# Four edits to a planned kernel: PSUM tags of the GT batches, one copy on another engine, later offers of denominators' and M's pieces

## The chip, the cores and the metric

The kernel runs on one core of a Trainium2 chip. The metric is the device time of one execution in microseconds. TensorE (PE) multiplies, VectorE (DVE) and ScalarE (ACT) work element by element, SyncE (SP) and GpSimd (POOL) here issue almost nothing but DMAs. TensorE writes into PSUM alone, which has eight banks; the kernel uses them as four pairs, called ch, dd, cc and rot.

## The reference

A gated mix of two blocks over 2048 tokens of 640 features, all in fp32:

```python
g = sigmoid((x * gate_w).sum(-1, keepdims=True))
# A: linear attention, 32 heads of 20
q, k, v = split(x @ wqkv)
phi = lambda t: where(t > 0, t + 1, exp(t)) + 1e-6
num = phi(q) @ (phi(k)^T v)              # per head
den = phi(q) @ sum_s(phi(k)) + 1e-6      # per head
a = (num / den) @ wo
# B: gated linear unit, F = 1536
b = (sigmoid(x @ w_gate) * (x @ w_up)) @ w_down
out = g * a + (1 - g) * b
```

## The kernel before

**Arithmetic.** Every fp32 operand is split into a high and a low part, and a product is made of three TensorE products, high by high, low by high and high by low (`mm3`, lines 406 to 408 of the profile). A split takes a ScalarE copy (the high part, L419) and a VectorE subtraction (the low part, L423). Larger products use sums of blocks in Strassen's manner (steps s1 to s7), so VectorE also makes sums of tiles.

**Stages, in order of time.** Up to 143 us the keys phi(k) are computed in four chunks of tokens, and the batches of GT = x^T phi(k) are summed into the SBUF tile `gt`. From 143 to 190 us come the queries of the second half of the tokens, and beside them kv = v^T-weight times GT per group of heads (`kv_part`) and M = kv times wo (`m_part`), in six parts hg of 0 to 5. A part of M is two products of 320 columns into two buffers of one PSUM pair, each copied to the tile `ms`, and one store to `m_dram` by POOL's queue. From 190 to 425 us follows the B block for the second half of the tokens, whose weights are split on the way and stored for later; from 425 us the queries and the B block of the first half; from 650 us on the A block's last product, phi(q) / den times M.

**GT batches.** A batch (`GTBatch`) has ten units u, of 128 x 320 outputs each, and up to four token tiles. `part(u, t0, t1, tag)` takes a PSUM buffer of the pair `tag` if the unit has none yet, adds tiles t0 to t1, and, behind the last tile, lets VectorE add the result to `gt`. `ps_tile(tag)` hands out the two buffers of a pair in turn, so the third unit of one tag waits until the first is added. The batches for c of 1, 2 and 3 begin some units earlier, between products of the keys, with two of their four tiles (units 0 to 4 for c of 1, 0 to 3 for c of 2 and 3, in rot, dd, ch and cc); the loop over all ten units then completes them.

**The planner.** The order of every engine's instructions is fixed while the program is built. `Order` keeps an estimated clock for TensorE (`pe`), ScalarE (`act`) and VectorE (`vec`), estimates of when each tile is written and read, and, in `Ring`, of when each DMA lands. Work that isn't tied to a place is offered with `order.add(a, v, fn, key, ready, ...)`: its cost on ScalarE and VectorE, the function that issues it, and a function that says from when it is ready. `order.fill()`, called between products and ahead of each PSUM copy, issues such work while it is ready and its end lies at most a slack behind `pe` (0.6 us for ScalarE, 1.2 for VectorE; 1.6 and 2.4 in some stages). There are several queues: urgent, streams with due times, items, lazy, chain and spare; of the last four only the head may go. `order.need(key)` issues everything up to a key at once. `order.when(tile)` is the estimated time of the tile's last writing, for a DMA its landing. Nothing of this exists at run time: an instruction issued too early simply waits in its engine's queue, and what stands behind it waits too.

**Denominators.** During the B block of the first half, `queue_dens` makes den in a chain for two groups of 512 tokens at a time, queued at block f of 3 (groups 2 and 3) and of 7 (groups 0 and 1). For each group, five pieces `pden` of phi(q) are loaded from `p_dram` by SP, two ahead, and VectorE adds each, times a column of z, to `fac` (`one`, L434 for the first, L427 for the others). Then `fac` goes to `den_dram`, comes back turned (`turn_in`), becomes gate / den (`factor`), goes to `fac_dram` and comes back (`turn_out`). `queue_scale` multiplies with it in the A block.

**M's pieces.** From the end of block 2 of that phase on, `queue_m` loads one of five pieces of M from `m_dram` into the tile `mr` by SP, four DMAs each, splits it into `mt`, and stores it to `mp_dram` by POOL; only then is the next piece queued. They are the spare queue. At block 9 `order.need("m")` makes sure that all are done; then `load_ms` loads into `mt` and `mr` again.

**Down pairs.** In blocks f of 3, 5, 7, 9 and 11 of each B phase, `down_pair` multiplies the gated activations of two blocks (`hf`) by the down weights (`wf` or `wd`), into rot, dd, ch and cc, each output added to `tb` by VectorE (in the first pair copied by ScalarE where `tb` has nothing yet).

Of the kernel before, what the change touches and what calls it, by code (L numbers as in the profile page):

```python
# [9 lines left out]
AF = mybir.ActivationFunctionType  # L10
# [5 lines left out]
S, D, F = 2048, 640, 1536  # L16
H, DH = 32, 20
KC = D // P
# [3 lines left out]
HALF = D // 2  # L22
# [344 lines left out]
def a_cost(w):  # L367
    return 0.06 + w / 1200

def v_cost(w):  # L370
    return 0.07 + w / 960

@with_exitstack
def gated_mix_kernel(ctx: ExitStack, tc: tile.TileContext, xt, xn, wk, wv, wo, wst_q, wst_f, out_t):
# [6 lines left out]
    order = Order()  # L381
# [3 lines left out]
    def f32(ap):  # L385
        return ap.bitcast(F32)

    def width(ap):
        n = 1
        for s in ap.shape[1:]:  # L390
            n *= s
        return n
# [7 lines left out]
    def ps_tile(tag):  # L400
        t = ps_borrow(tag)
        ps_turn[tag] = 1 - ps_turn.get(tag, 0)
        return t

    def mm3(out, l_hi, l_lo, r_hi, r_lo, first, last):
        nc.tensor.matmul(out, l_hi, r_hi, start=first, stop=False, skip_group_check=True)  # L406
        nc.tensor.matmul(out, l_hi, r_lo, start=False, stop=False, skip_group_check=True)  # L407
        nc.tensor.matmul(out, l_lo, r_hi, start=False, stop=last, skip_group_check=True)  # L408
        order.mm(out, width(out), first, l_hi, r_hi)
        order.mm(out, width(out), False, l_hi, r_lo)  # L410
        order.mm(out, width(out), False, l_lo, r_hi)
# [5 lines left out]
    def act(out, src, fn, after="", **kw):  # L417
        order.on_act(width(out), after, out, src)
        nc.scalar.activation(out, src, fn, **kw)  # L419

    def vec2(out, a, b, op, after=""):
        order.on_vec(width(out), after, 1.0, out, a, b)
        nc.vector.tensor_tensor(out, a, b, op=op)  # L423

    def vec3(out, a, scalar, b, op0, op1, after=""):
        order.on_vec(width(out), after, 1.0, out, a, b)
        nc.vector.scalar_tensor_tensor(out, a, scalar, b, op0=op0, op1=op1)  # L427

    def vec1(out, a, s0, s1=None, op0=OP.mult, op1=None, after=""):
        order.on_vec(width(out), after, 1.0, out, a)  # L430
        if op1 is None:
            nc.vector.tensor_scalar(out, a, s0, None, op0=op0)
        else:
            nc.vector.tensor_scalar(out, a, s0, s1, op0=op0, op1=op1)  # L434

    def split(hi, lo, src, after=""):
        act(hi, src, AF.Copy, after)
        at = order.act + A_LAG

        def low():  # L440
            order.vec = max(order.vec, at)
            vec2(lo, src, f32(hi), OP.subtract)
        order.then(low)

    def add(out, a, b, after=""):
        vec2(out, a, b, OP.add, after)
# [10 lines left out]
    fac = common.tile([P, NG, TG], F32, name="fac")  # L457
# [23 lines left out]
    def m1_tile(tag, name, dt=F32, rows=P):  # L481
        return m1.tile([rows, D], dt, name=name, tag=tag, bufs=2 if tag == "ma" else 3)
# [313 lines left out]
    def vec_copy(out, src, after=""):  # L796
        order.on_vec(width(out), after, 1.0, out, src)
        nc.vector.tensor_copy(out, src)
# [222 lines left out]
    g = GTBatch(0, [0])  # L1021
# [8 lines left out]
    for c in range(1, 4):  # L1030
        ck = chunks[c]
        if c == 1:
# [14 lines left out]
            g = GTBatch(c, batches[c])  # L1047
# [97 lines left out]
        if c > 1:  # L1145
            g = GTBatch(c, batches[c])
# [17 lines left out]
            sp.dma_start(w_stage, wst_q[:, KC - 1])  # L1164
            queue_forms(nx)
        for u in range(2 * KC):
            g.part(u, 2 if u in g.ps else 0, 4, ("rot", "dd", "rot", "cc")[u % 4] if c == 3 else "rot")
            order.fill()
            if u in (3, 5, 7, 9,):
                order.run("qw")  # L1170
# [26 lines left out]
    def tt(name, dt=F32, shape=(P, TG)):  # L1197
        return pw.tile(list(shape), dt, name=name, tag="t", bufs=4)
# [202 lines left out]
    def queue_dens(*gs2):  # L1401

        st = {}

        def load(g, u):
            if u < KC:
                st[g, u] = tt("pden")
                sp.dma_start(st[g, u], p_dram[:, u, g])
                st["at", g, u] = lambda: order.when(st[g, u])

        def one(g, u):
            td = fac[:, g]
            if u == 0:
                vec1(td, st[g, u], zcol[:, 0:1], zeps[:, 0:1], OP.mult, OP.add)
            else:
                vec3(td, st[g, u], zcol[:, u:u + 1], td, OP.mult, OP.add)
            load(g, u + 2)
            if u == KC - 1:
                gp.dma_start(den_dram[:, g], td)
                st["at", g, u + 1] = lambda: order.when(den_dram[:, g])  # L1420

        def turn_in(g):
            for j in range(4):
                js = slice(j * H, (j + 1) * H)
                sp.dma_start(fac[js, g].rearrange("h (d c) -> h d c", c=P),
                                  den_dram[:, g, j * P:(j + 1) * P].rearrange("(d h) c -> h d c", h=H))
            st[g, "gs"] = tt("gs")[:, :P]
            sp.dma_start(st[g, "gs"], gate_rep[4 * g:4 * g + 4].rearrange("i h c -> (i h) c"))
            st["at", g, KC + 1] = lambda: max(order.when(fac[:, g]), order.when(st[g, "gs"]))

        def factor(g):
            td = fac[:, g]
            q = td[:, :P]
            add(td[:, :2 * P], td[:, :2 * P], td[:, 2 * P:])
            add(q, q, td[:, P:2 * P])
            order.on_vec(5 * P, "")
            nc.vector.reciprocal(q, q)
            vec2(q, q, st[g, "gs"], OP.mult)
            gp.dma_start(fac_dram[:, g], q)
            st["at", g, KC + 2] = lambda: order.when(fac_dram[:, g])  # L1440

        def turn_out(g):
            for d in range(4):
                sp.dma_start(fac[d * H:(d + 1) * H, g].rearrange("h (j c) -> h j c", c=P),
                                  fac_dram[:, g].rearrange("(j h) c -> h j c", h=H))
        order.add(0, 0, lambda: [load(g, u) for u in range(2) for g in gs2], chain=True)
        for u in range(KC):
            for g in gs2:
                order.add(0, v_cost(TG), lambda g=g, u=u: one(g, u), None, lambda g=g, u=u: st["at", g, u](), chain=True)
        for n, (v, fn) in enumerate(((0, turn_in), (2.0, factor), (0, turn_out))):  # L1450
            for g in gs2:
                order.add(0, v, lambda g=g, fn=fn: fn(g), ("fac", g) if n == 2 else None,
                          lambda g=g, n=n: st["at", g, KC + n](), chain=True)
# [7 lines left out]
    def hg_slice(hg):  # L1461
        h0, h1 = HG[hg:hg + 2]
        return h0 * DH, (h1 - h0) * DH
# [52 lines left out]
    def queue_wo(hg):  # L1516
        if hg < NHG:
            order.add(a_cost(D), v_cost(D), lambda: wo_split(hg), ("wo", hg), lambda: order.when(MO_AT[hg]), first=True)
# [17 lines left out]
    def m_part(hg, tag="cc"):  # L1536
        c0, w = hg_slice(hg)
        order.need(("wo", hg))
        (kvh, kvl), (woh, wol) = KV.pop(hg), WO.pop(hg)
        ms = m1_tile(("ma", "mb")[hg % 2], "ms", F32, bdn)  # L1540
        for h in range(2):
            ps = ps_tile(tag)
            cs = slice(h * HALF, (h + 1) * HALF)
            mm3(ps[:w, :HALF], kvh[:w, :w], kvl[:w, :w], woh[:w, cs], wol[:w, cs], True, True)
            act(ms[:w, cs], ps[:w, :HALF], AF.Copy, "p")
        gp.dma_start(m_dram[c0:c0 + w], ms[:w])
        queue_wo(hg + 2)

# [122 lines left out]
    def m_rows(dst, cols, queue, u=None):  # L1671

        for d in range(4):
            m = m_dram.rearrange("(h u d) n -> d h u n", u=KC, d=4)[d]
            queue.dma_start(dst[d * H:(d + 1) * H], m[:, u] if cols is None else m[:, :, cols])

    def queue_m(u=0):

        raw = down_pool[1].tile([P, D], F32, name="mr", tag="mr")
        m_rows(raw, None, sp, u)  # L1680

        def fn():
            t = down_pool[1].tile([P, 2, D], F32R, name="mt", tag="mt")
            split(t[:, 0], t[:, 1], raw)

            def rest():
                gp.dma_start(mp_dram[:, u], f32(t))
                if u + 1 < KC:
                    queue_m(u + 1)
            order.then(rest)  # L1690
        order.add(a_cost(D), v_cost(D), fn, "m", lambda: order.when(raw), spare=True)

    def m_close():
        nonlocal tb
# [499 lines left out]
    for hg, (j, t) in enumerate(((5, "cc"), (6, "dd"), (8, "dd"), (10, "dd"), (12, "dd"), (13, "dd"))):  # L2194
        extra[j].append(lambda hg=hg, t=t: m_part(hg, t))
# [427 lines left out]
```

## Time and profile before

| | us |
|---|---|
| median of 3 runs | 733.24 (733.22 to 734.12) |
| the profiled execution, whole | 733.22 |
| its span, first to last instruction | 731.3 |
| TensorE busy | 726.0 |
| VectorE busy | 561.3 |
| ScalarE busy | 358.4 |
| granted TensorE clock | 1.0 |

Rows in order of time give start, duration, engine, line, operation, output<-inputs, shape and count; in brackets is the idle time before the instruction and what ended it. Instructions of one kind that follow each other are merged into one row with a count. Rows of a tile give durations in ns as least/median/most, then the first and the last start in us. A row of waits gives the waiting engine and tile, what it waited for, the total in us, how many times, and the longest. A row of a stretch has its length, then busy us and instructions of PE, PEld (weight loads), DVE, ACT and POOL, the granted clock, the DMA share and GB/s. L406 to L408 are `mm3`'s three products, L419 any ScalarE activation, L423 any two-tensor VectorE operation, L427 its three-operand form, L798 a VectorE copy, L363 any DMA.

### The profile page before, as it was taken

Reading aid. Unit: us, or ns where it says so; the run is one execution under the profiler, and the core shown is the slowest. Engines: PE = TensorE matmul, PEld = TensorE weight load, DVE = VectorE, ACT = ScalarE, POOL = GpSimd, SP = SyncE. Lnnn points to the kernel's source line nnn. Section 1 sums busy time; section 2 is a strip of 40 time slices with the busy share of each in tenths; the row PEclk is TensorE's granted clock in tenths of the full one; section 3 lists DMA queues with packets and bytes.
Section 4 is the critical chain, followed back from the end, with each engine's and each line's share of the span. In section 5 each row is a group of like instructions: output and inputs, shape, how many; then the busy total and the mean of one; then the engine's idle time right before and its main releaser. Section 6 shows DMA issues by size and latency. Waiting matters only on the chain.

```text
span 731.3 us, 10111 instructions
## 1 busy us (share of the span) xinstructions
PE 726.0 (99%) x3575; PEld 622.6 (85%) x3575; DVE 561.3 (77%) x987; ACT 358.4 (49%) x668; POOL 94.7 (13%) x161
## 2 busy tenths in 40 slices
PE   9999999999999999999999999999999999999997
PEld 7999999988888888888888888887888888888886
DVE  4978787987677889898989973456685867698783
ACT  5765647357556653535355363454333232334550
POOL 0211111113211211211210031001000041000000
PEclk9999999999999999999999999999999999999999
DMA  7564747697887866457687288878879697859212
GB/s 260 131 187 123 188 112 240 157 348 273 285 297 259 329 240 234 187 216 261 251 324 264 103 289 331 310 257 296 284 271 334 213 325 211 297 217 340 82 63 102
DMA packets 71945, 173.54 MB, mean 237 GB/s; under 512 B 11690, under 2 KB 33466, under 8 KB 68310
## 3 DMA queue, kind: packets, MB, share of 16 engines
q1 hardware_dynamic: 55526, 109.99, 45.6%
q0 software_dynamic: 16224, 62.74, 24.3%
q8 instruction: 28, 0.46, 0.2%
q14 instruction: 23, 0.19, 0.1%
q10 hardware_dynamic: 144, 0.16, 0.1%
HBM read 103.96 MB, written 63.92 MB: 230 GB/s over the span
## 4 chain that ended last, share of the span: by engine, by line
PE 85%; DVE 5%; DMA 4%; issue 2%; ACT 2%; POOL 1%; SPq 0%; DVEq 0%; POOLq 0%; ACTq 0%
PE ch L406 9%; PE ch L407 9%; PE ch L408 9%; PE cc L406 8%; PE cc L408 8%; PE cc L407 8%; PE dd L406 6%; PE dd L407 6%; PE dd L408 6%; PE rot L406 5%; PE rot L408 5%; PE rot L407 5%; DMA wo_sb<-wo 1%; DMA pden<-p_dram 1%; DVE gt L423 1%
## 5 line engine op out<-in xcount | busy, mean ns | idle before, releaser
L419 ACT ACTIVATE c<-ch 128x512 f32<-128x512 f32 x52 | 31.0, 597 | 94.0 <-PE ch L408 93.8
L423 DVE TENSOR_TENSOR hf<-c,hf 128x512 fp32r<-128x512 f32 x75 | 51.1, 687 | 25.5 <-ACT hf L419 25.0
L419 ACT ACTIVATE hf<-c 128x512 fp32r<-128x512 f32 x75 | 46.0, 624 | 26.7 <-DVE c L423 26.6
L423 DVE TENSOR_TENSOR c<-cc,c 128x512 f32<-128x512 f32 x40 | 27.6, 689 | 38.6 <-PE cc L408 24.8
L406 PE MATMUL ch<-xth,ws 128*128 128x512 f32 x112 | 43.7, 390 | 0.0
L407 PE MATMUL ch<-xtl,ws 128*128 128x512 f32 x112 | 43.6, 389 | 0.0
L408 PE MATMUL ch<-xth,ws 128*128 128x512 f32 x112 | 43.6, 389 | 0.0
L423 DVE TENSOR_TENSOR tb<-rot,tb 128x512 f32<-128x512 f32 (+1 forms) x61 | 39.2, 672 | 3.0 <-PE rot L408 3.0
L423 DVE TENSOR_TENSOR tb<-dd,tb 128x512 f32<-128x512 f32 x44 | 30.1, 685 | 8.7 <-PE dd L408 8.7
L406 PE MATMUL dd<-xrh,wg 128*128 128x512 f32 x90 | 35.2, 391 | 0.0
L408 PE MATMUL dd<-xrh,wg 128*128 128x512 f32 x90 | 35.0, 389 | 0.0
L407 PE MATMUL dd<-xrl,wg 128*128 128x512 f32 x90 | 35.0, 389 | 0.0
L423 DVE TENSOR_TENSOR c<-c,c 128x512 f32<-128x512 f32 x46 | 31.6, 687 | 2.6 <-ACT c L419 2.0
L419 ACT ACTIVATE c<-dd 128x512 f32<-128x512 f32 x22 | 13.1, 597 | 41.7 <-PE dd L408 41.5
L407 PE MATMUL cc<-xbl,ws 128*128 128x512 f32 x84 | 32.7, 389 | 0.0
L406 PE MATMUL cc<-xbh,ws 128*128 128x512 f32 x84 | 32.7, 389 | 0.0
L408 PE MATMUL cc<-xbh,ws 128*128 128x512 f32 x84 | 32.7, 389 | 0.0
L419 ACT ACTIVATE dd<-ch 128x512 f32<-128x512 f32 x22 | 12.8, 582 | 33.4 <-PE ch L408 33.4
L423 DVE TENSOR_TENSOR wst<-wst 128x256 f32<-128x256 f32 (+2 forms) x69 | 27.4, 412 | 1.4
L406 PE MATMUL rot<-pkh,xnh 128*128 128x320 f32 x90 | 28.1, 312 | 0.1
L407 PE MATMUL rot<-pkl,xnh 128*128 128x320 f32 x90 | 27.8, 309 | 0.0
L408 PE MATMUL rot<-pkh,xnl 128*128 128x320 f32 x90 | 27.8, 309 | 0.0
(648 smaller groups left out, 2327.8 us busy)
## 6 DMA issues: line engine op xcount, KB each, us to landing
wf<-ws POOLq DMA_DIRECT2D x12, 1152.0 KB, 7.6
ws<-wf SPq DMA_DIRECT2D x11, 1152.0 KB, 8.4
wst<-wst_f SPq DMA_DIRECT2D x12, 640.0 KB, 5.1
wf<-wg POOLq DMA_DIRECT2D x12, 640.0 KB, 6.7
wd<-wd POOLq DMA_DIRECT2D x12, 640.0 KB, 8.3
wg<-wf SPq DMA_DIRECT2D x12, 640.0 KB, 5.5
wf<-wd SPq DMA_DIRECT2D x10, 640.0 KB, 9.3
xnst<-xn SPq DMA_DIRECT2D x16, 320.0 KB, 4.1
```

The lines of the kernel that those rows point to most:

```text
L406: nc.tensor.matmul(out, l_hi, r_hi, start=first, stop=False, skip_group_check=True)
L407: nc.tensor.matmul(out, l_hi, r_lo, start=False, stop=False, skip_group_check=True)
L408: nc.tensor.matmul(out, l_lo, r_hi, start=False, stop=last, skip_group_check=True)
L419: nc.scalar.activation(out, src, fn, **kw)
L423: nc.vector.tensor_tensor(out, a, b, op=op)
```

## The change

In the loop over the ten units, batches for c of 1 and 2 now take their tags in turn from rot, dd, rot, cc for units under 8, as the batch for c of 3 did for all ten; units that have a buffer already keep it. The fifth part of M (hg of 4) is copied out of PSUM by VectorE, both halves; the other five parts stay with ScalarE. A denominators' piece is offered 1.5 us behind the modelled landing of its load, the factor 2.5 us behind the modelled landing of its two inputs, a piece of M 2 us behind that of its load.

```diff
         for u in range(2 * KC):
-            g.part(u, 2 if u in g.ps else 0, 4, ("rot", "dd", "rot", "cc")[u % 4] if c == 3 else "rot")
+            g.part(u, 2 if u in g.ps else 0, 4, ("rot", "dd", "rot", "cc")[u % 4] if c == 3 or u < 8 else "rot")
             order.fill()
...
                 sp.dma_start(st[g, u], p_dram[:, u, g])
-                st["at", g, u] = lambda: order.when(st[g, u])
+                st["at", g, u] = lambda: order.when(st[g, u]) + 1.5
...
-            st["at", g, KC + 1] = lambda: max(order.when(fac[:, g]), order.when(st[g, "gs"]))
+            st["at", g, KC + 1] = lambda: max(order.when(fac[:, g]), order.when(st[g, "gs"])) + 2.5
...
             mm3(ps[:w, :HALF], kvh[:w, :w], kvl[:w, :w], woh[:w, cs], wol[:w, cs], True, True)
-            act(ms[:w, cs], ps[:w, :HALF], AF.Copy, "p")
+            if hg == 4:
+                vec_copy(ms[:w, cs], ps[:w, :HALF], "p")
+            else:
+                act(ms[:w, cs], ps[:w, :HALF], AF.Copy, "p")
         gp.dma_start(m_dram[c0:c0 + w], ms[:w])
...
-        order.add(a_cost(D), v_cost(D), fn, "m", lambda: order.when(raw), spare=True)
+        order.add(a_cost(D), v_cost(D), fn, "m", lambda: order.when(raw) + 2, spare=True)
```

## The prediction

> **What bounds the kernel now.** I read the head of the page first, then TensorE's list of waits, then the table by stretches, and then the order of time around each wait.
>
> ```profile
> span 731.3 us, 10111 instructions
> PE 726.0 (99%) x3575; PEld 622.6 (85%) x3575; DVE 561.3 (77%) x987; ACT 358.4 (49%) x668; POOL 94.7 (13%) x161
> ```
> ```profile
> PE rot L494 <- PEq L2614: 0.8, 1, 0.8
> PE rot L406 <- DVE tb L423: 0.4, 1, 0.4
> PE dd L406 <- ACT ms L419: 0.2, 1, 0.2
> ```
> ```profile
> 625.00:732.00 107.00, 102.59 (x467) 85.33 (x465) 78.19 (x129) 41.74 (x78) 0.00 (x0) 1.00 0.49 175
> ```
>
> TensorE is the bound. It is idle for 731.3 - 726.0 = 5.3 us: 0.8 before its first product, some 3.7 behind its last one (625.00 to 731.3 is 106.3 us, of which it is busy 102.59), and the rest in a few waits. No product is added or dropped, so the change can gain only what TensorE loses in waits, and it can lose time only by making new ones. Since busy spans overlap and are modelled, I measure a wait by the distance from one start to the next, against that distance where nothing waits. The profiled execution took 733.22 us, 0.02 below the median of the runs (733.24), so its span and the 1.9 us around it can be used as they are.
>
> **GT batches in four banks.** Only units 5 and 7 of the second and third batch (c of 1 and 2) get another tag: the first batch has a loop of its own, for c of 3 the four tags are there already, units 0 to 3 have their buffer by then, and 4 and 6 keep rot.
>
> ```profile
> 62.83 0.31 PE L407 MATMUL rot<-pkl,xnh 128*128 128x320 f32 x1
> 62.98 0.31 PE L408 MATMUL rot<-pkh,xnl 128*128 128x320 f32 x1
> 63.41 0.41 PE L406 MATMUL rot<-pkh,xnh 128*128 128x320 f32 x1
> 63.66 0.31 PE L407 MATMUL rot<-pkl,xnh 128*128 128x320 f32 x1
> ```
> ```profile
> 58.63 0.48 DVE L423 TENSOR_TENSOR gt<-rot,gt 128x320 f32<-128x320 f32 x1
> ...
> 62.27 0.69 DVE L423 TENSOR_TENSOR xst<-xst 128x512 f32<-128x512 f32 x1
> 62.87 0.48 DVE L423 TENSOR_TENSOR gt<-rot,gt 128x320 f32<-128x320 f32 x1
> ```
>
> The regular distance is 62.98 - 62.83 = 0.15 us. At 63.41 unit 8 of the batch for c = 1 begins, after 0.43 instead, and its second product after 0.25: 0.28 + 0.10 = 0.38 us lost. It waits for a rot buffer. There are two, so unit 8 takes the one of unit 6, whose add stands on VectorE behind an x sum and starts only at 62.87. With the new tags unit 5 goes to dd and unit 7 to cc; unit 8 then takes the buffer of unit 4, added at 58.63, and unit 9 that of unit 6, added by 63.35, when unit 8 is just begun. The dd and cc buffers come free at adds that stand ahead of these in program order. VectorE's work stays the same, and what is next late is the x forms of the following chunk. I count the whole 0.38. The batch for c = 2 shows no wait: nothing to gain, and what hides the edit is that its adds keep up.
>
> **M's fifth part copied by VectorE.**
>
> ```profile
> 178.69 0.31 PE L408 MATMUL dd<-woh,kvl 100*100 100x320 f32 x1
> 180.21 0.39 PE L407 MATMUL ch<-xtl,ws 128*128 128x512 f32 x1
> 180.44 0.40 PE L408 MATMUL ch<-xth,ws 128*128 128x512 f32 x1
> 181.04 0.39 PE L406 MATMUL dd<-woh,kvh 100*100 100x320 f32 x1 [0.21 <-ACT ms L419]
> 181.27 0.31 PE L407 MATMUL dd<-wol,kvh 100*100 100x320 f32 x1
> ```
> ```profile
> 189.51 0.39 PE L406 MATMUL ch<-xth,ws 128*128 128x512 f32 x1
> ```
> ```profile
> 179.42 1.25 ACT L419 ACTIVATE ws<-wst 128x640 fp32r<-128x640 f32 x2
> 180.57 0.74 ACT L419 ACTIVATE ms<-dd 100x320 f32<-100x320 f32 x2
> ```
> ```profile
> 178.98 0.82 DVE L432 TENSOR_SCALAR zperm<-zacc 128x640 f32<-128x640 f32 x1
> 179.71 0.68 DVE L427 SCALAR_TENSOR_TENSOR qe<-qe,c 128x512 f32<-128x512 f32 x1
> 180.31 1.42 DVE L423 TENSOR_TENSOR ws<-wst,ws 128x640 fp32r<-128x640 f32 x2
> 181.84 0.69 DVE L423 TENSOR_TENSOR c<-cc,c 128x512 f32<-128x512 f32 x1
> 183.89 0.69 DVE L427 SCALAR_TENSOR_TENSOR qe<-qe,c 128x512 f32<-128x512 f32 x1 [1.36 <-ACT c L419]
> ```
> ```profile
> L798 DVE COPY gt<-dd x3: 475/477/479, 25.5 to 29.5; 128x320 f32<-128x320 f32 x3
> L419 ACT ACTIVATE gt<-dd x2: 437/438/438, 29.1 to 31.2; 128x320 f32<-128x320 f32 x2
> ```
>
> The regular distance here is 180.44 - 180.21 = 0.23, behind a 320-wide product 0.15. The sixth part starts after 0.60, and its second product after 0.23: 0.37 + 0.08 = 0.45 us lost. It waits for the copy of the fifth part's first half. That half's last product ended at 179.00, but its copy stands on ScalarE behind two weight splits until 180.57. On VectorE the two copies can stand ahead of the column permutation, from about 179.05 to 180.0, which frees the buffer some 0.7 us before it is wanted at 180.67. The price is two copies of 477 ns each, 0.95 us, against two of 438 on ScalarE. Behind them are queued the permutation, one phi step and the two halves of the ws low parts, which end at 181.73 now and at about 182.7 then. TensorE first reads that tile at 189.51, 6.8 us later, and VectorE's next gap of 1.36 us takes up the delay. The store of this part on POOL's queue goes out sooner, not later. So 0.45 gained, and nothing paid as long as those 6.8 us are there.
>
> The Trainium skill speaks against this edit: "Advanced Engine Details and Errata" says in its list of workarounds that ScalarE is the engine closer to PSUM, and "Perfetto Trace Analysis", section Optimizing Scalar/DVE Operations, gives about 125 ns of access overhead to a VectorE instruction on PSUM and about 51 to a ScalarE one. By that page two copies would cost 2 x 74 = 0.15 us more on VectorE, an estimate; the two gt rows above, the same shape on both engines, say 2 x 39 = 0.08 us. By either the sum is the same, because the copies lie beside TensorE's work.
>
> **Denominators' and M's pieces offered later.**
>
> ```profile
> 495.76 0.39 PE L408 MATMUL dd<-hf,wf 128*128 128x512 f32 x1
> 496.54 0.50 PE L406 MATMUL rot<-hf,wf 128*128 128x512 f32 x1 [0.39 <-DVE tb L423]
> 496.87 0.39 PE L407 MATMUL rot<-hf,wf 128*128 128x512 f32 x1
> ```
> ```profile
> 492.72 2.07 DVE L427 SCALAR_TENSOR_TENSOR fac<-pden,zcol,fac 128x512 f32<-128x512 f32 x3
> 495.13 0.75 DVE L427 SCALAR_TENSOR_TENSOR fac<-pden,zcol,fac 128x512 f32<-128x512 f32 x1 [0.34 <-DMA pden<-p_dram]
> 495.80 1.28 DVE L423 TENSOR_TENSOR tb<-rot,tb 128x512 f32<-128x512 f32 x2
> ```
> ```profile
> 497.97 0.74 ACT L419 ACTIVATE mt<-mr 128x640 fp32r<-128x640 f32 x1 [4.59 <-DMA mr<-m_dram]
> ```
> ```profile
> L427 DVE SCALAR_TENSOR_TENSOR fac<-pden,zcol,fac x16: 739/744/752, 489.2 to 587.7; 128x512 f32<-128x512 f32 x16
> ...
> L363 SPq DMA_DIRECT2D fac<-fac_dram x16: 309/436/687, 540.1 to 621.1; - x16
> ...
> L427 DVE SCALAR_TENSOR_TENSOR hf<-hf,fac x10: 682/683/686, 669.6 to 676.0; 128x512 f32<-128x512 f32 x10
> ```
> ```profile
> L363 POOL DMA_DIRECT2D mt<-m_dram x8: 574/574/617, 589.4 to 596.0; - x8
> ...
> L363 POOL DMA_DIRECT2D mp_dram<-mt x5: 532/538/540, 492.5 to 538.0; - x5
> ```
> ```profile
> 591.92 0.39 PE L406 MATMUL dd<-hf,wf 128*128 128x512 f32 x1
> ```
>
> TensorE's longest wait inside the program: 0.78 against 0.23, then 0.33 against 0.23, so 0.55 + 0.10 = 0.65 us lost. The adds that free rot stand on VectorE behind four denominators' pieces, the last of which waits 0.34 us for its own load. Of the 0.65, 0.34 is that wait and the rest is the pieces themselves. Offered 1.5 us behind the modelled landing, a piece no longer holds VectorE for a load; whether the adds also come ahead of it is the planner's choice. Bounds: 0 (the pieces bunch elsewhere) to 0.65; I take 0.65, because each of the pieces ahead moves as well, the later ones by two such delays.
>
> What the delays push back: five rounds a group at 1.5 us are at most 7.5 us, and the factors 2.5 more, 10 us in all. The last turned factors are issued at 621.1 now, by 631 then, and first multiplied at 669.6. M's pieces: five at 2 us, so the last store goes from 538.0 to 548, and the mt tile is wanted again at 589.4. SP's loads of pieces and POOL's stores move with them; no weight load stands behind a wait that is longer than before, since SP issues the next piece's load when the piece has been used, and that now waits less. ScalarE's wait of 4.59 us at 497.97 shrinks by about 2, which gains nothing: TensorE runs on through it. One thing comes nearer: the second set's last piece starts at 587.7, and the next down pair, where a piece can stand before an add as at 496.54, begins at 591.92. A shift beyond some 3.5 us puts one or two pieces into it.
>
> The sum: 733.22 - 0.38 - 0.45 - 0.65 = 731.74 us.
>
> **Rivals.** *The denominators' wait only moves.* GT's and M's waits go, but one or two pieces fall before an add in this pair or in that at 591.92, at 0.65 each: 733.22 - 0.83 + 0 to 0.65 = 732.4 to 733.0. For it: the 7.5 us above against 3.5. Against it: a piece whose data is there costs 0.7 us of VectorE and not a wait, and behind an add it costs nothing.
>
> *Pieces bunch before the adds (slower).* The head of the chain is held back, and then several pieces are ready at once, as the three from 492.72 are, and go out where the planner thinks that VectorE has room. It reckons 512/960 + 0.07 = 0.60 us for a piece whose row says 0.74, so a bunch of four overruns by over 0.5 us. The twenty pieces pass through three down pairs. The estimate: with none of the 0.65 gained and five new waits of that size, 733.22 - 0.83 + 3.25 = 735.6. It decides from (0.83 + 1.47) / 0.65 = 3.5, so four waits on. Any other reordering that the changed estimates bring into the long middle part would have to cost as much. Against it: sixteen of the twenty pieces cost TensorE nothing before.
>
> *The edits don't reach the waits.* If the copies are placed on VectorE behind the ws low parts, or unit 8 still meets a full buffer, there is no change: 733.2.
>
> **How the numbers follow.** A measurement of this kernel can tell about 0.2% from no change, 1.47 us; the forecast gain of 1.48 lies on that line. All three waits go: 0.58, of which I put 0.44 beyond the line (small gaps also close) and 0.14 within. The wait only moves: 0.20, within. The edits miss: 0.02, within. Bunching: 0.20, slower. The time is that of the first case, 731.7. The range goes from 731.2 (0.5 below it: the runs before spread over 0.9) to 734.4, which takes in the second and third rival and bunching with three new waits (732.4 + 1.95); the rest of bunching is left out.
>
> **What would show it.** Right: TensorE's list of waits keeps only the start; two 100x320 copies by VectorE from about 179; no VectorE wait on pden; the last M store near 545, the last turned factors before 635. Wrong: a TensorE wait on tb or gt anywhere between 480 and 625, or new waits between 182 and 480, where there are none.

## The result and the profile after

| | before | after |
|---|---|---|
| median of 12 runs each, us | 733.65 (733.19 to 735.91) | 731.78 (731.41 to 732.20) |
| the profiled execution, whole | 733.22 | 731.51 |
| its span | 731.3 | 729.6 |

The ratio is 0.9972, with an interval of 0.9963 to 0.9981: faster by 1.87 us, against a forecast of 1.48. Run again beside the later experiments, the change took 731.80 against 734.14, a ratio of 0.9967 [0.9955, 0.9980].

The head of the page after, and the whole of TensorE's list of waits:

```profile
span 729.6 us, 10115 instructions
PE 725.0 (99%) x3575; PEld 623.4 (85%) x3575; DVE 562.3 (77%) x989; ACT 357.8 (49%) x666; POOL 94.9 (13%) x161
```
```profile
PE rot L494 <- PEq L2617: 0.8, 1, 0.8
```

VectorE has two instructions more and ScalarE two fewer, the two copies of M's fifth part. TensorE's products are the same 3575, and of the three waits only the start is left. The three places of the prediction, in TensorE's order of time:

```profile
62.70 0.31 PE L408 MATMUL cc<-pkh,xnl 128*128 128x320 f32 x1
62.84 0.31 PE L406 MATMUL rot<-pkh,xnh 128*128 128x320 f32 x1
62.99 0.31 PE L407 MATMUL rot<-pkl,xnh 128*128 128x320 f32 x1
...
179.78 0.39 PE L408 MATMUL ch<-xth,ws 128*128 128x512 f32 x1
180.01 0.32 PE L406 MATMUL dd<-woh,kvh 100*100 100x320 f32 x1
180.17 0.31 PE L407 MATMUL dd<-wol,kvh 100*100 100x320 f32 x1
...
494.74 0.39 PE L408 MATMUL dd<-hf,wf 128*128 128x512 f32 x1
494.97 0.39 PE L406 MATMUL rot<-hf,wf 128*128 128x512 f32 x1
495.19 0.39 PE L407 MATMUL rot<-hf,wf 128*128 128x512 f32 x1
```

The distances are now the regular ones: 0.14 and 0.15 us at unit 8 of the batch, 0.23 and 0.16 at M's sixth part, 0.23 and 0.22 at the product into rot. With the products of both traces put side by side, start against start, the gain grows as follows: 0.28 us by the time of 30 us, where no edit has acted yet (this differs from one execution to the next); 0.38 more at unit 8; 0.45 more at M's sixth part, of which 0.06 is given back just behind it; 0.66 more near 495. From there to the end it stays between 1.68 and 1.72, and the two spans differ by 1.71.

What VectorE does at the second of these places:

```profile
178.38 0.93 DVE L798 COPY ms<-dd 100x320 f32<-100x320 f32 x2
179.23 0.82 DVE L432 TENSOR_SCALAR zperm<-zacc 128x640 f32<-128x640 f32 x1
179.96 0.69 DVE L427 SCALAR_TENSOR_TENSOR qe<-qe,c 128x512 f32<-128x512 f32 x1
180.56 1.43 DVE L423 TENSOR_TENSOR ws<-wst,ws 128x640 fp32r<-128x640 f32 x2
...
183.95 0.69 DVE L427 SCALAR_TENSOR_TENSOR qe<-qe,c 128x512 f32<-128x512 f32 x1 [1.36 <-ACT c L419]
```

The copies stand ahead of the permutation, as supposed, and the ws low parts end at 181.99, far ahead of their reading; the gap of 1.36 us ahead of the phi step (L427) is as long as before. And at the third:

```profile
487.55 1.22 DVE L434 TENSOR_SCALAR fac<-pden,zcol,zeps 128x512 f32<-128x512 f32 x2 [1.57 <-DMA pden<-p_dram]
...
490.29 1.41 DVE L427 SCALAR_TENSOR_TENSOR fac<-pden,zcol,fac 128x512 f32<-128x512 f32 x2
491.92 0.75 DVE L427 SCALAR_TENSOR_TENSOR fac<-pden,zcol,fac 128x512 f32<-128x512 f32 x1 [0.22 <-DMA pden<-p_dram]
492.98 0.75 DVE L427 SCALAR_TENSOR_TENSOR fac<-pden,zcol,fac 128x512 f32<-128x512 f32 x1 [0.31 <-DMA pden<-p_dram]
493.65 1.28 DVE L423 TENSOR_TENSOR tb<-rot,tb 128x512 f32<-128x512 f32 x2
```

The kernel before began this stretch so:

```profile
487.75 1.22 DVE L434 TENSOR_SCALAR fac<-pden,zcol,zeps 128x512 f32<-128x512 f32 x2 [0.76 <-DMA pden<-p_dram]
489.18 0.75 DVE L427 SCALAR_TENSOR_TENSOR fac<-pden,zcol,fac 128x512 f32<-128x512 f32 x1 [0.21 <-DMA pden<-p_dram]
490.71 0.75 DVE L427 SCALAR_TENSOR_TENSOR fac<-pden,zcol,fac 128x512 f32<-128x512 f32 x1 [0.78 <-DMA pden<-p_dram]
```

Before, six pieces by L427 stood between the two first ones (L434) and the two rot adds: those at 489.18 and 490.71, three from 492.72 and one at 495.13. Now there are four. The adds begin at 493.65 instead of 495.80; 1.02 of these 2.15 us had been gained ahead of this place, and the other 1.13 are more than the 0.55 that TensorE stood waiting, so TensorE finds its buffer free. VectorE still waits for loads: the brackets in the rows after show 1.57, 0.22 and 0.31 us.

From the answers by tile, for pden (first before, then after), fac, mt and ms:

```profile
  DMA pden<-p_dram: 2.1, 4
```
```profile
  DMA pden<-p_dram: 2.1, 3
```
```profile
L363 SPq DMA_DIRECT2D fac<-fac_dram x16: 309/430/1082, 538.4 to 619.0; - x16
```
```profile
L363 POOL DMA_DIRECT2D mp_dram<-mt x5: 534/540/540, 490.1 to 538.3; - x5
```
```profile
L419 ACT ACTIVATE ms<-dd x8: 420/436/442, 164.2 to 181.1; 100x320 f32<-100x320 f32 x6, 120x320 f32<-120x320 f32 x2
L798 DVE COPY ms<-dd x2: 492/493/494, 178.4 to 178.8; 100x320 f32<-100x320 f32 x2
```

The first two rows say that VectorE's waits on pden come to 2.1 us before and after, in 4 places and in 3. The last turned factors are issued at 619.0 (621.1 before) and the last store of M at 538.3 (538.0 before). TensorE is 1.7 us ahead of the kernel before by then, so against its work the factors come 0.4 us sooner and the store 2.0 later; both are far from the 10 us that were reckoned.

### The profile page after: what moved, and what is told of

The parts are those of the page before. It is cut to its first block, busy times and chain, and to the rows that moved or that the text cites. A ratio compares the mean times of both kernels' runs of the same rounds, so it can differ in the third digit from the quotient of the medians.

```text
span 729.6 us, 10115 instructions
## 1 busy us (share of the span) xinstructions
PE 725.0 (99%) x3575; PEld 623.4 (85%) x3575; DVE 562.3 (77%) x989; ACT 357.8 (49%) x666; POOL 94.9 (13%) x161
## 4 chain that ended last, share of the span: by engine, by line
PE 99%; DVE 0%; issue 0%
PE ch L406 11%; PE ch L407 11%; PE ch L408 11%; PE cc L406 9%; PE cc L407 9%; PE cc L408 9%; PE dd L406 8%; PE dd L407 8%; PE dd L408 8%; PE rot L406 6%; PE rot L407 6%; PE rot L408 6%; PE rot L1525 1%; PE rot L494 0%; PE ch L965 0%; PE dd L965 0%
## 5 line engine op out<-in xcount | busy, mean ns | idle before, releaser
L408 PEld LDWEIGHTS ch<-xth,ws 128*128 128x128 f32 x112 | 21.0, 188 | 4.7 <-DVE ws L423 0.3
L407 PEld LDWEIGHTS ch<-xtl,ws 128*128 128x128 f32 x112 | 21.0, 188 | 4.2
L406 PEld LDWEIGHTS ch<-xth,ws 128*128 128x128 f32 x112 | 21.0, 188 | 4.1
```

## The experiments

Twelve kernels in three groups, each group timed beside the kernel before (medians 734.17, 734.26 and 734.14). What TensorE lost at each place in the profiled execution, in us, worked out from distances of starts as in the prediction:

| | GT unit 8 | M | near 496 | near 518 | near 530 | span |
|---|---|---|---|---|---|---|
| before | 0.38 | 0.46 | 0.66 | 0 | 0 | 731.3 |
| GT alone | 0 | 0.47 | 0.89 | 0 | 0 | 731.6 |
| M's fifth part alone | 0.38 | 0.02 | 1.96 | 0 | 0 | 731.8 |
| denominators alone | 0.39 | 0.46 | 0 | 0.78 | 1.39 | 732.7 |
| M's pieces alone | 0.44 | 0.47 | 1.59 | 0.28 | 0 | 732.6 |
| denominators and M's pieces | 0.38 | 0.46 | 0 | 0 | 0 | 731.0 |
| all but M's pieces | 0 | 0.02 | 0 | 0 | 1.11 | 731.3 |
| all | 0 | 0.01 | 0 | 0 | 0 | 729.6 |

The spans hold something else besides: from TensorE's start to the first GT product the executions take 21.5 to 22.4 us, a difference of up to 0.9, so they are no measure of a few tenths.

### GT's tags alone

```diff
-            g.part(u, 2 if u in g.ps else 0, 4, ("rot", "dd", "rot", "cc")[u % 4] if c == 3 else "rot")
+            g.part(u, 2 if u in g.ps else 0, 4, ("rot", "dd", "rot", "cc")[u % 4] if c == 3 or u < 8 else "rot")
```

> Only the GT batches' tags are changed, all else as before. Theory (each edit removes one wait, and they add up): the wait at unit 8 of the batch for c = 1 goes, 0.38 us, the waits near 181 and 496 stay; 0.4 us faster than before, no new wait. Rival (VectorE is the bound in that batch and the wait only moves): a TensorE wait on another PSUM pair or on an x form between 63 and 75 us, no gain.

Measured: 733.37 us, ratio 0.9990 [0.9979, 1.0002]. The interval includes 1, so the time alone doesn't show the forecast 0.4 us. In the trace the wait at unit 8 goes from 0.38 to 0, and no other appears between 63 and 75 us. The profiled execution loses this gain again: 0.21 us at 160.5, where the kernel before loses nothing and the profile names no releaser, and 0.23 at the wait near 496, which is longer here (TensorE's order of time):

```profile
495.74 0.39 PE L408 MATMUL dd<-hf,wf 128*128 128x512 f32 x1
496.75 0.50 PE L406 MATMUL rot<-hf,wf 128*128 128x512 f32 x1 [0.62 <-DVE tb L423]
```

### M's fifth part alone

```diff
-            act(ms[:w, cs], ps[:w, :HALF], AF.Copy, "p")
+            if hg == 4:
+                vec_copy(ms[:w, cs], ps[:w, :HALF], "p")
+            else:
+                act(ms[:w, cs], ps[:w, :HALF], AF.Copy, "p")
```

> Only M's fifth part is copied by VectorE. Theory: the wait near 181 us goes, 0.45 us faster than before, VectorE's copies start about when the products end and the weights' low parts end some 1 us later without TensorE noticing. Rival (a copy on VectorE costs more there than it saves, because what is queued behind it is late): gain under 0.2 us, with a TensorE wait between 181 and 195.

Measured: 733.70 us, ratio 0.9999 [0.9989, 1.0008]. The wait at M's sixth part goes, 0.46 to 0.02, and yet no gain shows in the time; the interval would hide one of up to 0.8 us, so the trace has to say where it went. TensorE's and VectorE's order of time near 496:

```profile
494.97 0.39 PE L408 MATMUL dd<-hf,wf 128*128 128x512 f32 x1
497.05 0.50 PE L406 MATMUL rot<-hf,wf 128*128 128x512 f32 x1 [1.69 <-DVE tb L423]
```
```profile
488.54 1.21 DVE L434 TENSOR_SCALAR fac<-pden,zcol,zeps 128x512 f32<-128x512 f32 x2 [2.34 <-DMA pden<-p_dram]
...
496.31 1.28 DVE L423 TENSOR_TENSOR tb<-rot,tb 128x512 f32<-128x512 f32 x2
```

TensorE comes to the last product into dd 0.8 us sooner than before (494.97 against 495.76; about half of it is this edit, the rest the start of this execution) and starts the next one 0.5 us later (497.05 against 496.54). VectorE has stood waiting for its first pieces until 488.54, 0.79 later than before, and the adds are 0.51 later (496.31 against 495.80). In this execution the end of the wait is set by loads, not by how early TensorE comes.

### The denominators' delays alone

```diff
-                st["at", g, u] = lambda: order.when(st[g, u])
+                st["at", g, u] = lambda: order.when(st[g, u]) + 1.5
...
-            st["at", g, KC + 1] = lambda: max(order.when(fac[:, g]), order.when(st[g, "gs"]))
+            st["at", g, KC + 1] = lambda: max(order.when(fac[:, g]), order.when(st[g, "gs"])) + 2.5
```

> Only the denominators' pieces and factors are offered later (1.5 and 2.5 us). Theory: the wait near 496 us goes, 0.65 us faster than before, because fewer pieces stand ahead of the two adds into tb on VectorE. Rival (M's pieces hold VectorE and ScalarE there): the wait stays at 0.4 us or more.

Measured: 734.24 us, ratio 0.9997 [0.9987, 1.0008]. The wait near 496 is gone, and two others have come: 0.78 us near 518, of which the list of waits puts 0.4 on a weight load (`wf<-wd`), and 1.39 near 530. The second, in the order of time of TensorE, ScalarE and VectorE:

```profile
529.72 0.39 PE L408 MATMUL cc<-hf,wf 128*128 128x512 f32 x1
531.23 0.50 PE L406 MATMUL rot<-hf,wf 128*128 128x512 f32 x1 [1.11 <-DVE tb L423]
```
```profile
528.38 0.74 ACT L419 ACTIVATE mt<-mr 128x640 fp32r<-128x640 f32 x1 [5.18 <-DMA mr<-m_dram]
```
```profile
529.15 0.83 DVE L423 TENSOR_TENSOR mt<-mr,mt 128x640 fp32r<-128x640 f32 x1 [2.39 <-ACT mt L419]
...
530.49 1.28 DVE L423 TENSOR_TENSOR tb<-rot,tb 128x512 f32<-128x512 f32 x2
```

A piece of M is split ahead of the rot adds. ScalarE waits 5.18 us for its load, VectorE 2.39 for ScalarE, the adds stand behind that, and TensorE waits for the adds.

### M's pieces' delay alone

```diff
-        order.add(a_cost(D), v_cost(D), fn, "m", lambda: order.when(raw), spare=True)
+        order.add(a_cost(D), v_cost(D), fn, "m", lambda: order.when(raw) + 2, spare=True)
```

> Only M's pieces are offered later (2 us). Theory: TensorE never waited for them, and six denominators' pieces still stand ahead of the two adds: the wait near 496 us stays at 0.5 to 0.7 us and the time is that of before within 0.1 us. Rival (the split of M's piece is what holds the adds up): the wait shrinks by half or more, 0.3 to 0.6 us faster.

Measured: 737.84 us (734.33 to 739.04), ratio 1.0048 [1.0033, 1.0063]: slower, which no theory gave. Its profiled execution was the fastest of its runs, 734.33, and shows 1.59 us near 496, as in the old order, and 0.28 near 518. Against the kernel before these are 1.2 us more, about what the two profiled executions differ by (1.1). There are six runs instead of twelve. The other 3.5 us, from this execution to the median, were not seen in a trace, and what they are stays open.

### Denominators' and M's pieces together, without the first two edits

```diff
-                st["at", g, u] = lambda: order.when(st[g, u])
+                st["at", g, u] = lambda: order.when(st[g, u]) + 1.5
...
-        order.add(a_cost(D), v_cost(D), fn, "m", lambda: order.when(raw), spare=True)
+        order.add(a_cost(D), v_cost(D), fn, "m", lambda: order.when(raw) + 2, spare=True)
```

(and the factor's 2.5)

> Both kinds of offers later (denominators' 1.5 and 2.5 us, M's pieces 2 us), GT tags and M's fifth part as before. Theory after the first runs (the two work only together: the first empties VectorE's queue ahead of the adds near 496, the second keeps a split of M's piece out of the next down pair, where it held an add for 1.4 us at 530): no TensorE wait between 480 and 560, 0.7 to 1.5 us faster than before, and a spread over the runs under 1.5 us. Rival (each acts alone, as at first thought): the wait at 530 is there again and nothing is gained.

Measured: 732.49 us, ratio 0.9971 [0.9957, 0.9985]. No wait of TensorE from 480 to 560, and the runs lie within 1.0 us. Alone, the one edit gives nothing that can be measured and the other loses; together they gain 1.8 us.

### The whole change without the delay of M's pieces

```diff
-        order.add(a_cost(D), v_cost(D), fn, "m", lambda: order.when(raw) + 2, spare=True)
+        order.add(a_cost(D), v_cost(D), fn, "m", lambda: order.when(raw), spare=True)
```

> The whole change without the later offer of M's pieces. Theory: GT's and M's waits are gone (0.37 and 0.4 us), the wait near 496 too, but a split of M's piece stands ahead of two adds near 530 and costs 1 to 1.5 us: slower than the whole change by 1 to 2 us, at the time of before or up to 0.5 us under it. Rival (M's offers don't matter): the time of the whole change within 0.3 us.

Measured: 732.89 us, ratio 0.9977 [0.9965, 0.9990], about 1.1 us above the whole change (731.80, in the third group, where the kernel before took 734.14 instead of 734.26). The intervals of the two ratios overlap, so the times alone don't decide it; the traces do. TensorE and VectorE near 530, first of this kernel, then VectorE of the whole change:

```profile
529.80 0.50 PE L406 MATMUL rot<-hf,wf 128*128 128x512 f32 x1 [0.83 <-DVE tb L423]
```
```profile
527.72 0.83 DVE L423 TENSOR_TENSOR mt<-mr,mt 128x640 fp32r<-128x640 f32 x1 [2.11 <-ACT mt L419]
...
529.07 1.28 DVE L423 TENSOR_TENSOR tb<-rot,tb 128x512 f32<-128x512 f32 x2
```
```profile
527.01 1.28 DVE L423 TENSOR_TENSOR tb<-rot,tb 128x512 f32<-128x512 f32 x2
```

With the 2 us the piece of M goes to another place, and the adds come 2.06 us sooner; 0.51 of that is the whole change's lead in its own execution. The loss near 530 is in both profiled kernels that delay the denominators without M's pieces (1.39 and 1.11 us) and in none that delays both. So the delay that the prediction counted at nothing is what keeps the denominators' gain.

### Only unit 5, or only unit 7, on another pair

Each kernel was run once, so there is no interval, and the reading rests on the order in the trace. In both, the batch for c of 3 stays as it was.

```diff
+ only unit 5: ("rot", "dd", "rot", "cc")[u % 4] if c == 3 else "dd" if u == 5 else "rot"
+ only unit 7: ("rot", "dd", "rot", "cc")[u % 4] if c == 3 else "cc" if u == 7 else "rot"
```

> Of the whole change only unit 5's tag in the GT batches for c = 1 and 2 (to dd). Unit 8 then still takes the buffer of unit 6. By the prediction's account (the buffer alone decides) the wait at unit 8 stays at some 0.4 us. Rival: the planner also puts unit 6's add ahead of the x sum on VectorE, a microsecond earlier, and that alone removes the wait.

> Of the whole change only unit 7's tag in the GT batches for c = 1 and 2 (to cc). Unit 8 then takes the buffer of unit 5, and unit 6's add stays behind the x sum. By the prediction's account the wait at unit 8 goes, 0.38 us. Rival (only the earlier add helps): it stays.

With unit 5 alone (one run, 733.85 us) unit 8 still takes the buffer of unit 6, and still doesn't wait. VectorE and TensorE:

```profile
62.31 0.48 DVE L423 TENSOR_TENSOR gt<-rot,gt 128x320 f32<-128x320 f32 x1
62.71 1.41 DVE L423 TENSOR_TENSOR xst<-xst 128x512 f32<-128x512 f32 x2
```
```profile
63.19 0.31 PE L408 MATMUL rot<-pkh,xnl 128*128 128x320 f32 x1
63.33 0.31 PE L406 MATMUL rot<-pkh,xnh 128*128 128x320 f32 x1
```

The planner has put unit 6's add ahead of the x sums, at 62.31 instead of 62.87, and that is enough. With unit 7 alone (one run, 733.53) the add stays behind an x sum, and unit 8 takes the other buffer:

```profile
61.81 0.68 DVE L423 TENSOR_TENSOR xst<-xst 128x512 f32<-128x512 f32 x1
62.41 0.48 DVE L423 TENSOR_TENSOR gt<-rot,gt 128x320 f32<-128x320 f32 x1
```
```profile
62.53 0.31 PE L408 MATMUL cc<-pkh,xnl 128*128 128x320 f32 x1
62.67 0.31 PE L406 MATMUL rot<-pkh,xnh 128*128 128x320 f32 x1
```

Unit 8 starts 0.14 behind the product ahead of it, at 62.67, while that add is still running. Either means alone is enough.

### The change again

> The whole change again, beside the runs of this job. Theory: the three waits stay gone in every run, so the spread is under 1.5 us, and the ratio to before is 0.996 to 0.998; before's runs spread wider because the landing of the denominators' loads near 490 differs from run to run.

Measured: 731.80 us (731.40 to 732.56), profiled 731.75, span 729.8, TensorE losing nothing at the five places of the table but 0.02 at M.

### Denominators' pieces offered 4 us late

```diff
-                st["at", g, u] = lambda: order.when(st[g, u]) + 1.5
+                st["at", g, u] = lambda: order.when(st[g, u]) + 4
```

> The whole change, with denominators' pieces offered 4 us behind their modelled landing instead of 1.5. Theory: VectorE's waits on these loads (2.1 us in the profile before) fall under 0.7, one piece stands between the two adds near 494, TensorE doesn't wait, and the time is that of the whole change within 0.4 us. Rival (the prediction's slower case: pieces held back bunch ahead of the adds of the down pairs): TensorE waits on tb between 490 and 610, 0.6 us each, 0.6 to 2 us slower than the whole change.

Measured: 731.70 us, ratio 0.9958 [0.9945, 0.9971], the same as the whole change. From the answers on pden and fac:

```profile
  DMA pden<-p_dram: 0.4, 1
```
```profile
L427 DVE SCALAR_TENSOR_TENSOR fac<-pden,zcol,fac x16: 739/744/748, 491.6 to 597.7; 128x512 f32<-128x512 f32 x16
```

VectorE waits 0.4 us for these loads instead of 2.1, and the last piece starts at 597.7, within the pair that begins near 590 here (591.92 before). TensorE has no wait either way. So pieces in that pair cost nothing here, they don't bunch to a loss, and VectorE's wait on pden is not itself what costs: it did so only where the adds stood behind it and TensorE had come to their buffer.

### All six parts of M copied by VectorE

```diff
-            if hg == 4:
-                vec_copy(ms[:w, cs], ps[:w, :HALF], "p")
-            else:
-                act(ms[:w, cs], ps[:w, :HALF], AF.Copy, "p")
+            vec_copy(ms[:w, cs], ps[:w, :HALF], "p")
```

> The whole change, with all six parts of M copied by VectorE. Theory (the fifth part gains only because ScalarE's queue is full there and VectorE's is not): ten more copies of 0.48 us make VectorE late somewhere between 155 and 195, a TensorE wait of 0.3 to 2 us in all, slower than the whole change by as much. Rival (VectorE is simply the better engine for this copy): no new wait, the time of the whole change within 0.3 us.

Measured: 732.47 us (731.63 to 734.24), ratio 0.9975 [0.9961, 0.9989]. The stretch from 155 to 195 us of the whole change and of this kernel:

```profile
155.00:195.00 40.00, 40.00 (x213) 34.30 (x212) 29.57 (x56) 28.17 (x52) 12.08 (x22) 1.00 0.90 319
```
```profile
155.00:195.00 40.00, 40.00 (x212) 33.94 (x211) 33.82 (x68) 24.85 (x42) 12.08 (x22) 1.00 0.90 311
```

VectorE is busy for 33.82 of the 40 us instead of 29.57, and TensorE for all 40 in both. The list of waits has nothing new, and the span is 729.8, but the order of time holds one small wait of the expected kind. VectorE's add of a cc buffer into c runs from 182.25 to 182.93, where the whole change has it from 181.90 to 182.59. The first product into that pair starts at 182.99, lasts 0.50 us instead of 0.39, and the next follows after 0.33 instead of 0.23: 0.15 us lost, against 0.3 to 2 expected. So VectorE's lead is just used up there. The median is 0.67 above the whole change, with a wider spread and overlapping intervals; what makes up the rest isn't settled.

### The first GT batch in four pairs too

The first batch waits as well: its units start late near 30 and 31 us, 0.41 us in all in the profile after.

```diff
-                g.part(u, 0, 2, "rot" if u % 2 else "dd")
+                g.part(u, 0, 2, ("dd", "rot", "ch", "cc")[u % 4])
```

> The whole change, and the first GT batch, too, turns in four PSUM pairs (dd, rot, ch, cc instead of dd and rot). Theory: the two waits left there, near 30 and 31 us (0.2 to 0.3 and 0.17 us), go: 0.3 to 0.5 us faster than the whole change. Rival (what is behind those waits is late too): the wait moves to the key products that follow at 32, no gain.

Measured: 731.46 us (730.92 to 733.21), ratio 0.9962 [0.9948, 0.9975]. The waits near 30 and 31 us are gone, 0.41 to 0.00; in its profiled execution 0.30 is lost near 519, for which the list of waits names no cause. By its median it is the fastest of all, 0.34 below the change, but the intervals don't tell the two apart.

## Why the prediction was right, and where it was not

**GT, 0.38.** Measured 0.38. The account, that the buffer decides, is half of it: an earlier place of unit 6's add does the same with the buffer unchanged (the run with unit 5 alone), and VectorE's order after the whole change has both:

```profile
61.82 0.48 DVE L423 TENSOR_TENSOR gt<-rot,gt 128x320 f32<-128x320 f32 x1
62.22 1.41 DVE L423 TENSOR_TENSOR xst<-xst 128x512 f32<-128x512 f32 x2
```

The prediction took VectorE's order as given where the new tags had moved it.

**M's fifth part, 0.45.** Measured 0.45, of which 0.06 is given back. The copies began at 178.38 and the low parts of ws ended at 181.99. Against the forecast of 179.05 and 182.7 that is 0.7 us sooner, but TensorE was 0.65 us ahead of the kernel before at that place: the forecast of the order was right to within 0.1. The two copies take 493 ns each against 436 on ScalarE, a difference of 57; with all six parts on VectorE ten such copies take 480 at the median, 44 more. The Trainium skill, "Perfetto Trace Analysis", section Optimizing Scalar/DVE Operations, gives 125 ns of access against 51, a difference of 74. The trace agrees in direction and comes out smaller, though the rows are whole durations and not the access alone. As the prediction said, by either the time is the same, since the copies lie beside TensorE's work. That holds for one part; with all six, 0.15 us of it reached TensorE.

**Denominators, 0.65.** Measured 0.66 between the two traces. But the size belongs to the one execution from which it was taken. Six profiled executions have the old order on VectorE at this place: the kernel before, GT's tags alone, M's fifth part alone, M's pieces alone, unit 5 and unit 7. TensorE was ready for this product at 495.2 to 496.0 us, and the product started at 496.5 to 497.4; the two earliest arrivals (495.2 and 495.3) started at 497.1 and 496.8, no sooner than the others. The loss was 0.66 in the kernel before and 0.89, 1.96, 1.59, 0.98 and 1.64 in the others. This is the term that was mis-sized for the median: the median gain was 1.87 and 2.34 us where the terms said 1.48. The kernel before was profiled once in these runs, in an execution of 733.22 at the low end of its spread (733.19 to 735.91); so that its usual wait is a longer one is likely from the five others, not shown. It also means that the three terms don't add as the sum had it. A wait whose end is set by loads swallows what was gained ahead of it: in the trace M's edit gives nothing while that wait stands, and its 0.45 only once it is gone. That rests on these traces, since the intervals of the single edits are too wide to show 0.4 us. What paces those loads stays open. That 731.78 came out within 0.04 us of 731.74 is partly luck: the sum started from an execution 0.43 us below the median of the kernel before, and the two profiled executions differ by 0.28 us where no edit acts.

**M's pieces, nothing.** Wrong. This was the step that failed, and the time came out right because it failed inside a whole that held. The prediction argued from ScalarE's wait of 4.59 us, which TensorE runs through; it did not ask where the pieces of M would go once the denominators' pieces had moved. Without the 2 us one of them stands before the adds near 530 and takes back 1.11 us. On their own the 2 us do harm, 0.48% by the ratio, most of it unexplained.

**What the delays push back.** Up to 10 us was reckoned; against TensorE's work it is -0.4 for the turned factors and +2.0 for M's last store. Offers of 1.5 us later have changed the order, but hardly the length of the chain; with 4 us the last turned factors are issued at 628.5, 9.5 us later than with 1.5, and that costs TensorE nothing either. The factor's 2.5 us do nothing at all: without them the planner gives the same instructions in the same order on every engine. The prediction also held that no weight load comes later. That is so in the whole change, but with the denominators delayed alone TensorE lost 0.78 us near 518, part of it to a weight load.

**What would show it.** TensorE's list and the two copies came as said. "No VectorE wait on pden" did not: 2.1 us before and after. The prediction's means, that a piece offered later no longer holds VectorE for its load, is not what happened: VectorE waits as long, but four pieces instead of six stand ahead of the adds. M's last store came at 538.3, not near 545. None of the signs of being wrong appeared.

**The rivals.** That the denominators' wait only moves is what happened in the two kernels without the delay of M's pieces, not in the pair at 591.92 but at 530, and by a piece of M, not of the denominators. With the whole change it did not happen. Bunching did not happen either, even at 4 us. The first case came, and the gain, 0.19 to 0.37% by the interval, lies on the line of 0.2% and beyond it, as reckoned.

## What to carry to other kernels

Read a short wait of the bound engine as the end of a queue: look at what stands ahead of the releasing instruction, and whether it in turn waits for a transfer, since such a wait will swallow every gain made ahead of it. When a delay or a cost in a planner is changed, ask of each kind of floating work where it goes once the other has moved, and try the edits together as well as one by one: here one of a pair gave nothing, the other lost half a per cent (most of it unexplained), and both gained 1.8 us. A single profile sizes such a transfer-paced wait badly; profile several programs that share the order before a sum rests on it.

## What the runs showed of the hardware

The loads that VectorE waits for near 490 don't come at the same time in every execution. Over six programs with the same order of instructions at this place, the adds behind them start at 495.80 to 496.61 us, and TensorE loses 0.66 to 1.96 us. Whether this also sets the spread of the runs is not shown. The two sets of the changed kernel spread over 0.8 and 1.2 us, against 2.7 or more before, but the kernels with all six parts of M on VectorE and with the first batch in four pairs, which don't have this wait either, spread over 2.6 and 2.3.

A product behind a wait costs more than the wait: near 496 and 530 it lasts 0.50 us instead of 0.39 at 512 columns, and the next one starts some 0.10 us late (0.33 instead of 0.23). Of the 0.65 us near 496, the list of waits names 0.39.
